# Turning k by 32 by 32 blocks on VectorE and sixteen transfers, in a hash attention kernel with a PReLU MLP behind it

## The chip, the cores and the metric

The kernel runs on one core of a Trainium2 chip. Its engines work side by side, each through its own instructions in order: TensorE (PE: matmuls, and PEld: the loads of their weights), VectorE (DVE), ScalarE (ACT), GpSimd (POOL) and SyncE (SP, which here only issues transfers). They meet through semaphores. Transfers are carried out by 16 DMA engines; an engine that issues one spends time on the issue and goes on, and whoever needs the data waits for the landing. The metric is the device time of one execution in microseconds (us), as the median of several runs. A profile is one execution, recorded instruction by instruction.

## The reference: hash attention, then a two-layer MLP

Four batches of eight heads, 768 positions, head dimension 64. Every q and k row is given six bits, the signs of its products with six columns of `proj`. A query may look only at keys with the same six bits; other scores become -1e9. Then softmax and the product with v. The heads of a batch are put side by side (512 columns) and go through `g = max(h, 0) + alpha * min(h, 0)` with `h = x @ w_in` (512 to 2048), and `out = g @ w_out`.

```python
q_bits = (np.einsum('bhsd,dk->bhsk', q, proj) > 0).astype(np.int64)
mask = q_bucket[:, :, :, None] == k_bucket[:, :, None, :]
scores = np.where(mask, scale * np.matmul(q, k.transpose(0, 1, 3, 2)), -1000000000.0)
```

## The kernel before, in words

Two heads make a pair; there are 16 pairs, and the loop at L1140 takes one per turn. Before the loop the first two pairs are loaded and turned. After it (`attn.close()`, L1201) comes the MLP, which the change does not touch.

Position `p * 6 + c` of a head lies in partition p as its row c, so a natural tile (`qn`, `kn`) holds 128 partitions of six rows of two heads of 64. TensorE needs the 128 numbers of both heads on the partitions and the 768 positions along the free axis. `turn` (L667) makes that: six 128x128 transposes by TensorE into two PSUM banks (L674), and one ScalarE copy out (L679), to `qT` or `kT`. The turned columns come in six groups of 128: group c holds the rows c of all partitions.

`hash_bits` (L687) multiplies the turned q and k by the projection (`hs`, L704), ScalarE's Sign (L710) turns them into `kb`, and six small transfers on SP's queue put the pieces of `kb` where the scores want them: four of 32 rows into `qb` (L715), two of 64 rows within `kb` (L717). `scores` (L734) computes, for each of twelve cells (six groups of keys by two halves of the queries), the bits' product and the score on top of it in one PSUM tile; the weights are 128 columns of `kb` and `kT`, the moving side 384 columns of `qb` and `qT`. ScalarE's exponential (L745) empties the tile into `pt`. `attend` (L767) multiplies `pt` by v into `av`. Meanwhile VectorE adds up the six `pt` tiles (L753, 761, 757, 758, 764), `totals` (L781) sums the partitions with TensorE (`sm`), and `divide` (L794) divides: it runs within the next pair and stores x to DRAM (L823).

In the same loop the MLP's weights are prepared: ScalarE makes `wr` and `wx` of a loaded `raw` piece (`weight_abs`, L580 and L584), VectorE clamps, shifts and adds them (L590, L596, L621, L624), and in some pairs subtracts finished groups (`weight_sums`, L642). Finished groups go back to DRAM (L634, L647). `magnitude` (L681) squares q and k in place and keeps the sum, for a check of range; it is the last use of a natural tile, after which `load` (L499) fills it anew.

The order on TensorE, VectorE, ScalarE and GpSimd is the program's: nearly every instruction is passed to `do`, which keeps it there. Transfers issued on SP are placed by the tile layer by their dependencies. In one turn pi the order is: the scores of pair pi with their exponentials; the division of the pair before; weight work and the sums of `pt`; `hash_bits` of pair pi+1; `turn` of q and of k of pair pi+2; `attend` and `totals` of pi; one `weight_abs`; loads; `magnitude` of q and k of pair pi, each followed by the load for pair pi+3; a second `weight_abs`.

The PSUM tiles named `sc`, `tp`, `hs` and `sm` share three buffers of two banks. Natural tiles of q and k have three buffers each. Each transfer issued by SP or ScalarE takes one of eight semaphores in turn, and its issue waits until the transfer that had this semaphore before has landed.

Of the kernel before, what the change touches and what calls it, by code (L numbers as in the profile page):

```python
# [8 lines left out]
F32 = mybir.dt.float32  # L9
# [398 lines left out]
def fast_path(  # L408
# [12 lines left out]
    nc = tc.nc  # L421
    P = 128
    B, H, S, D = q.shape
# [5 lines left out]
    NC = S // P  # L429
    NK = DM // P  # L430
    NF = DFF // P
    CH = 3
# [44 lines left out]

    pts = [pool.tile([P, NCH, 2, CW + 1], F32, name=f"pt{i}", bufs=1) for i in range(NC)]

    nat, tr, bits = {}, {}, {}  # L480
    accp, accd, av, vsum, sums = {}, {}, {}, {}, {}

# [10 lines left out]
    def load_part(pi, name, cs, queue):  # L493
        b, hp = pairs[pi]
        src = {"q": q, "k": k}[name]
        if cs.start == 0:
            nat[name, pi] = pool.tile([P, NC, 2, D], F32, name=f"{name}n{pi}", tag=f"{name}n", bufs=3)
        for s in range(2):
            queue.dma_start(nat[name, pi][:, cs, s], src[b, 2 * hp + s].rearrange("(p c) d -> p c d", c=NC)[:, cs])  # L499

# [166 lines left out]
    def turn(pi, name, halves=BOTH, engine=None):  # L667
# [10 lines left out]
        else:  # L678
            do(ACT.activation(dst, ps[:, halves, :CW], AF.Copy, scale=DOWN if name == "q" else 1.0))  # L679

    def magnitude(pi, name):  # L681

        t = nat[name, pi].rearrange("p c h d -> p (c h d)")
        n = "qk".index(name)
        do(ACT.activation(t, t, AF.Square, accum_out=mags[:, n, pi : pi + 1]))

    def hash_bits(pi, halves=BOTH, engine=None):  # L687

        if halves.start == 0:
            bits["q", pi] = qbs[pi % 2]
            kb = pool.tile([P, 3 * CW], BF16, name=f"kb{pi}", tag="kb", bufs=1)
            bits["k", pi] = kb[:, :S]
            bits["raw", pi] = kb.rearrange("p (a w) -> p a w", w=CW)
        ps = {"k": two_banks(f"hs{pi}")}
        ps["q"] = psum_av.tile([P, 2, 512], F32, name=f"hsq{pi}", tag="av") if engine is DVE else ps["k"]
        for half in range(halves.start, halves.stop):
            for name in "qk" if engine is DVE else "kq":
                for s in range(2):  # L700
                    r, c = D * s, D * (s ^ half) + 32 * "kq".index(name)

                    for t, c in [("k", c)] + ([("q", c ^ D)] if engine is DVE and name == "q" else []):
                        do(PE.matmul(  # L704
                            ps[t][c : c + 32, half if t == "k" or engine is not DVE else 0, :CW], wh[r : r + D],
                            tr[name, pi][r : r + D, half * CW : (half + 1) * CW], start=True, stop=True,
                        ))
        if engine is None:
            raw = bits["raw", pi]
            do(ACT.activation(raw[:, 0:3:2], ps["k"][:, :, :CW], AF.Sign, bias=hb))  # L710
            for half in range(2):
                for s in range(2):
                    c = D * (s ^ half)
                    cols = slice(half * CW, (half + 1) * CW)
                    nc.sync.dma_start(bits["q", pi][D * s : D * s + 32, cols], raw[c + 32 : c + 64, 2 * half])  # L715
                    if half:
                        nc.sync.dma_start(bits["k", pi][D * s : D * s + D, cols], raw[c : c + D, 2])  # L717
            return
        for half in range(halves.start, halves.stop):
            cols = slice(half * CW, (half + 1) * CW)  # L720
            for s in range(2):
                c = D * (s ^ half ^ (engine is DVE)) + 32
                do(ACT.activation(
                    bits["q", pi][D * s : D * s + 32, cols], ps["q"][c : c + 32, 0 if engine is DVE else half, :CW], AF.Sign, bias=hb[c : c + 32],
                ))

            for to, c, n in [(0, 0, P)] if half == 0 else [(0, D, D), (D, 0, D)]:
                dst, src = bits["k", pi][to : to + n, cols], ps["k"][c : c + n, half, :CW]
                do(DVE.tensor_scalar(
                    dst, src, hb_k[c : c + n, 0:1], hb_k[c : c + n, 1:2], op0=ALU.is_gt, op1=ALU.subtract,  # L730
                ))


    def scores(pi, cells):  # L734
        for kc, g in cells:
            sc = two_banks(f"sc{pi}_{kc}_{g}")
            ks = slice(kc * P, (kc + 1) * P)
            qs = slice(g * CW, (g + 1) * CW)
            for what, first in ((bits, True), (tr, False)):
                for s in range(2):  # L740
                    r = slice(D * s, D * s + D)
                    do(PE.matmul(  # L742
                        sc[:, s, :CW], what["k", pi][r, ks], what["q", pi][r, qs], start=first, stop=not first,
                    ))
            do(ACT.activation(pts[kc][:, g, :, :CW], sc[:, :, :CW], AF.Exp, scale=SCALE / DOWN))  # L745

# [393 lines left out]
    for pi in range(NPAIR):  # L1140
        i = 2 * pi

        def weight_begin():
            weight_clamp(i)
            weight_parts(i)
            add_first(pi)

        scores(pi, [c for c in CELLS if pi or c not in ahead])
        if pi:
            divide(pi - 1, weight_begin)  # L1150
        else:
            add_first(pi)
        weight_sum(i)
        weight_group(i)
        load_weight(i + 3)
        if pi == 0:
            weight_abs(1, DVE)
        weight_clamp(i + 1)
        add_third(pi)
        add_last(pi)  # L1160
        weight_parts(i + 1)
        weight_sum(i + 1)
        weight_group(i + 1)
        load_weight(i + 4)
        add_total(pi)
        weight_sums(2)
        if pi + 1 < NPAIR:
            hash_bits(pi + 1)
        if pi + 2 < NPAIR:
            turn(pi + 2, "q")  # L1170
            turn(pi + 2, "k")
        attend(pi)
        if pi + 1 == NPAIR:
            now = ff1(0, 0)
            now.step(1)
# [12 lines left out]
        if 11 <= pi < 14 or pi == 15:  # L1188
            sum_x(0, min(pi - 11, 3), DVE)
        if pi == 1:  # L1190
            setup_alpha()
        for name in "qk":
            magnitude(pi, name)
            if pi + 3 < NPAIR:
                load(pi + 3, name)
        if pi + 1 < NPAIR:
            weight_abs(i + 3)
# [97 lines left out]
```

## Time and profile before

| | |
|---|---|
| median of three runs | 897.62 us (896.51 to 897.95) |
| the profiled execution | 897.64 us, its span 895.8 us |
| TensorE clock granted | 0.997 |
| busy in the span: PE, PEld, DVE, ACT | 884.2, 598.5, 746.8, 379.5 us |
| attention stage | up to about 341 us |
| first exponential of pairs 1, 8, 9, 10, 11, 14, 15 | 33.04, 178.92, 199.52, 220.13, 240.74, 303.16, 324.11 us |
| chain that ended last | PE 84%, DVE 9%, issue 3%, ACT 2%, DMA 2% |

A row of a group reads: line, engine, operation, tile written from tile read, shapes, count, then busy time in us and the mean of one in ns. A row of a timeline reads: start and duration in us, engine, line, operation, tiles, count, and in brackets how long the engine was idle before and who ended that. Times count from the start of the span. `issue` stands for waiting that no recorded instruction explains. The rows of SPq are its issues, not the data's way.

### The profile page before, as it was taken

To read this page: it belongs to the slowest core of one execution; us is meant where nothing else is said; L and a number is where in the kernel's file an instruction comes from. 1 tells how busy PE (TensorE), PEld (TensorE's weight loads), DVE (VectorE), ACT (ScalarE), POOL (GpSimd) and SP (SyncE) were. 2 spreads that over 40 slices of the span, in tenths; PEclk is the share of its full clock that TensorE was granted. 3 is DMA by queue.
4 is the path that set the end of the run, shared out by engine and by line. 5 is a ranking of instruction groups with operands and counts; after the bars stand their busy time and mean duration, and the time that the engine had idled before them with its cause. 6 is when DMAs were issued, how large, how long until landed. Compare 5 with 4: busy or idle time off the path is not lost.

```text
span 895.8 us, 15331 instructions
## 1 busy us (share of the span) xinstructions
PE 884.2 (99%) x5886; PEld 598.5 (67%) x5886; DVE 746.8 (83%) x1266; ACT 379.5 (42%) x668; POOL 14.4 (2%) x30
## 2 busy tenths in 40 slices
PE   9999999999999999999999999999999999999996
PEld 4544545555555545557997557997557998556996
DVE  5888888888989887899989678988668989768996
ACT  7877777788877762222112222112222111222111
POOL 1000000000000001120000000000000000000000
PEclk9999999999999999999999999999999999999998
DMA  8444575575685625587333435343525242430242
GB/s 235 139 143 129 151 232 153 149 229 173 204 281 163 202 74 185 181 296 289 141 113 107 163 111 166 107 147 88 178 88 192 95 159 80 157 116 0 95 143 72
DMA packets 126177, 137.22 MB, mean 153 GB/s; under 512 B 78976, under 2 KB 110224, under 8 KB 122512
## 3 DMA queue, kind: packets, MB, share of 16 engines
q1 hardware_dynamic: 121376, 126.59, 44.9%
q0 software_dynamic: 2304, 8.39, 2.6%
q10 hardware_dynamic: 2416, 1.18, 0.5%
q8 instruction: 48, 0.79, 0.3%
q14 instruction: 33, 0.27, 0.1%
HBM read 104.87 MB, written 28.31 MB: 149 GB/s over the span
## 4 chain that ended last, share of the span: by engine, by line
PE 84%; DVE 9%; issue 3%; ACT 2%; DMA 2%; SPq 0%; DVEq 0%; ACTq 0%
PE sc L742 12%; PE av L775 10%; PE f_0a L875 2%; PE z_4a L875 2%; PE z_7a L875 2%; PE z_3a L875 2%; PE z_6a L875 2%; PE z_5a L875 2%; PE f_4a L875 2%; PE f_3a L875 2%; PE f_2a L875 2%; PE f_1a L875 2%; PE z_2a L875 2%; PE f_5a L875 2%; DMA qb<-kb 2%
## 5 line engine op out<-in xcount | busy, mean ns | idle before, releaser
L745 ACT ACTIVATE pt<-sc 128x768 f32<-128x768 f32 x192 | 154.8, 812 | 53.5 <-PE sc L742 53.2
L742 PE MATMUL sc<-qT,kT 64*128 64x384 f32 x768 | 155.8, 483 | 0.0
L775 PE MATMUL av<-pt,vn 128*32 128x385 f32 (+1 forms) x1536 | 127.4, 486 | 0.0
L742 PEld LDWEIGHTS sc<-qT,kT 64*128 64x128 f32 x768 | 70.0, 187 | 40.9 <-issue 40.7
L775 PEld LDWEIGHTS av<-pt,vn 128*32 128x32 f32 x1536 | 48.7, 109 | 71.1 <-issue 70.5
L928 DVE TENSOR_TENSOR g<-g,g 128x384 f32<-128x384 f32 x128 | 68.4, 555 | 2.2
L742 PE MATMUL sc<-qb,kb 64*128 64x384 bf16 x384 | 66.5, 323 | 2.4 <-DMA qb<-kb 2.1
L992 DVE TENSOR_TENSOR gs<-g,gs 128x768 f32<-128x768 f32 x56 | 53.3, 952 | 1.0
L992 DVE TENSOR_TENSOR gs<-g 128x768 f32<-128x768 f32 x56 | 53.3, 951 | 0.0
L984 DVE TENSOR_TENSOR ws<-wl 128x512 f32<-128x512 f32 x56 | 38.5, 687 | 17.5 <-DMA wl<-w_out_s 15.9
L753 DVE TENSOR_TENSOR accp<-pt,pt 128x1536 f32<-128x1536 f32 x16 | 28.1, 1759 | 17.5 <-ACT pt L745 17.5
L924 DVE SCALAR_TENSOR_TENSOR g<-h,alpha 128x384 f32<-128x384 f32 x32 | 19.7, 616 | 25.1 <-ACT h L917 25.1
L742 PEld LDWEIGHTS <-kb 64*128 64x128 bf16 x384 | 20.9, 94 | 25.9 <-issue 4.3
L580 ACT ACTIVATE wr<-raw 128x512 int32<-128x512 uint32 x32 | 22.8, 712 | 17.2 <-issue 16.0
L758 DVE TENSOR_TENSOR accd<-accd,pt 128x1536 f32<-128x1536 f32 x16 | 28.1, 1759 | 2.0 <-ACT wr L580 0.5
L761 DVE TENSOR_TENSOR accp<-accp,pt 128x1536 f32<-128x1536 f32 x16 | 28.0, 1753 | 0.0
L757 DVE TENSOR_TENSOR accd<-pt,pt 128x1536 f32<-128x1536 f32 x16 | 28.0, 1752 | 0.0
L764 DVE TENSOR_TENSOR accd<-accd,accp 128x1536 f32<-128x1536 f32 x16 | 28.0, 1751 | 0.0
L805 DVE STREAM_TRANSPOSE st<-sm 128x192 f32<-128x192 f32 x32 | 10.3, 361 | 16.9 <-PE sm L789 16.9
L875 PE MATMUL f_0a<-x,wi 128*128 128x384 f32 x64 | 23.5, 489 | 0.0
L875 PE MATMUL f_4a<-x,wi 128*128 128x384 f32 x64 | 23.3, 486 | 0.0
L875 PE MATMUL f_1a<-x,wi 128*128 128x384 f32 x64 | 23.3, 486 | 0.0
(348 smaller groups left out, 1732.1 us busy)
## 6 DMA issues: line engine op xcount, KB each, us to landing
wi<-w_in_s SPq DMA_DIRECT2D x32, 896.0 KB, 4.7
wl<-w_out_s SPq DMA_DIRECT2D x16, 1024.0 KB, 4.8
wl<-w_out_r SPq DMA_DIRECT2D x12, 1024.0 KB, 4.9
raw<-in_moe_w_out_dram SPq DMA_DIRECT2D x16, 512.0 KB, 3.9
raw<-in_moe_w_in_dram SPq DMA_DIRECT2D x16, 512.0 KB, 4.0
w_in_s<-wsi SPq DMA_DIRECT2D x16, 448.0 KB, 5.8
vn<-in_v_dram SPq DMA_DIRECT2D x16, 384.0 KB, 4.2
x_s<-x SPq DMA_DIRECT2D x16, 384.0 KB, 2.8
```

The lines of the kernel that those rows point to most:

```text
L742: do(PE.matmul(sc[:, s, :CW], what["k", pi][r, ks], what["q", pi][r, qs], start=first, stop=not first,))
L745: do(ACT.activation(pts[kc][:, g, :, :CW], sc[:, :, :CW], AF.Exp, scale=SCALE / DOWN))
L753: do(DVE.tensor_tensor(accp[pi], p(0), p(1), op=ALU.add))
L757: do(DVE.tensor_tensor(accd[pi], p(3), p(4), op=ALU.add))
L758: do(DVE.tensor_tensor(accd[pi], accd[pi], p(5), op=ALU.add))
L761: do(DVE.tensor_tensor(accp[pi], accp[pi], p(2), op=ALU.add))
L764: do(DVE.tensor_tensor(accd[pi], accd[pi], accp[pi], op=ALU.add))
L775: do(PE.matmul(av[pi][D * s + t : D * s + t + 32, g, :w], nat["v", pi][:, s, kc * D + t : kc * D + t + 32], pts[kc][:, g, s, :w], start=(k ...
L875: do(PE.matmul(self.ps[bank], self.left(left, k), self.right(right, k), start=start and k == 0, stop=k == self.nk - 1, skip_group_check=no ...
L928: do(DVE.tensor_tensor(new_g(b, to)[:, i], g_m[b, x][:, i], g_m[b, y][:, i], op=ALU.subtract))
L984: do(DVE.tensor_tensor(t, w2[b, n, x], w2[b, n, y], op=op))
L992: do(DVE.tensor_tensor(t, g2[b, n, x], g2[b, n, y], op=ALU.subtract))
```

## The change

For pairs 2 to 15, k is no longer turned by TensorE. `turn_blocks` transposes the natural tile by VectorE in 32 by 32 blocks, in one instruction of 128x768, into a tile `kB` of one buffer (`tb`), and sixteen transfers on SP's queue move the blocks to `kT`, 32 partitions of 768 bytes each. The columns of such a `kT` stand in the order of the positions, so the group c is every sixth column; `columns` gives the scores this view, with a step of 24 bytes for `kT` and of 12 bytes for `kb`. `hash_bits` reads `kT` in order as before.

The six transfers of the hash bits are issued by ScalarE, directly after the Sign, in place of SP. Natural k tiles have two buffers in place of three. The square of k is that of pair pi+2 in turn pi (turn 0 does those of pairs 0, 1 and 2), so that the tile comes free early. The first two pairs are turned as before.

```diff
-            nat[name, pi] = pool.tile([P, NC, 2, D], F32, name=f"{name}n{pi}", tag=f"{name}n", bufs=3)
+            nat[name, pi] = pool.tile([P, NC, 2, D], F32, name=f"{name}n{pi}", tag=f"{name}n", bufs=2 if name in WITH_DVE else 3)
...
+    def turn_blocks(pi, name):
+        t = pool.tile([P, 4, 32, NC], F32, name=f"{name}B{pi}", tag="tb", bufs=1)
+        do(DVE.transpose(t.rearrange("p b i c -> p b c i"), nat[name, pi].rearrange("p c h (e d) -> p (h e) c d", d=32)))
+        w = NC * 32
+        tr[name, pi] = dst = pool.tile([P, S], F32, name=f"{name}T{pi}", tag=f"{name}T")
+        for a in range(4):
+            for b in range(4):
+                nc.sync.dma_start(
+                    dst[32 * b : 32 * b + 32, a * w : (a + 1) * w],
+                    t[32 * a : 32 * a + 32, b].rearrange("p i c -> p (i c)"),
+                )
+        by_blocks.add((name, pi))
...
+    def columns(what, name, pi, r, c0, c1):
+
+        t = what[name, pi][r]
+        if (name, pi) not in by_blocks:
+            return t[:, c0 * P : c1 * P]
+        t = t.rearrange("p (t c) -> p c t", c=NC)[:, c0:c1]
+        return t[:, 0] if c1 - c0 == 1 else t
...
-                    nc.sync.dma_start(bits["q", pi][D * s : D * s + 32, cols], raw[c + 32 : c + 64, 2 * half])
+                    do(nc.scalar.dma_start(bits["q", pi][D * s : D * s + 32, cols], raw[c + 32 : c + 64, 2 * half]))
                     if half:
-                        nc.sync.dma_start(bits["k", pi][D * s : D * s + D, cols], raw[c : c + D, 2])
+                        do(nc.scalar.dma_start(bits["k", pi][D * s : D * s + D, cols], raw[c : c + D, 2]))
...
-                        sc[:, s, :CW], what["k", pi][r, ks], what["q", pi][r, qs], start=first, stop=not first,
+                        sc[:, s, :CW], columns(what, "k", pi, r, kc, kc + 1),
+                        columns(what, "q", pi, r, CH * g, CH * (g + 1)), start=first, stop=not first,
...
+        if pi == 0:
+            for name in WITH_DVE:
+                magnitude(0, name)
...
-            turn(pi + 2, "k")
+            turn_blocks(pi + 2, "k")
...
-            magnitude(pi, name)
+            for n in [1, 2] if pi == 0 and name in WITH_DVE else [pi + 2 * (name in WITH_DVE)]:
+                if n < NPAIR:
+                    magnitude(n, name)
```

More of the change, by code (lines that the diff above doesn't have):

```diff
@@ L478, in fast_path @@
     pts = [pool.tile([P, NCH, 2, CW + 1], F32, name=f"pt{i}", bufs=1) for i in range(NC)]
+    WITH_DVE = "k"
     nat, tr, bits = {}, {}, {}
@@ L679, in turn @@
             do(ACT.activation(dst, ps[:, halves, :CW], AF.Copy, scale=DOWN if name == "q" else 1.0))
+    def turn_blocks(pi, name):
[10 more added lines that the diff above has]
+        by_blocks.add((name, pi))
+    by_blocks = set()
+    def columns(what, name, pi, r, c0, c1):
[4 more added lines that the diff above has]
+        return t[:, 0] if c1 - c0 == 1 else t
     def magnitude(pi, name):
@@ L736, in scores @@
             sc = two_banks(f"sc{pi}_{kc}_{g}")
-            ks = slice(kc * P, (kc + 1) * P)
-            qs = slice(g * CW, (g + 1) * CW)
             for what, first in ((bits, True), (tr, False)):
```

## The prediction

> **What bounds the kernel now.** I read the page first, for the busy engines, then the tables by stage, the chain of waits, and last the timelines of one pair on four engines, since the change lives wholly in the attention stage (up to 341 us).
>
> ```profile
> PE 884.2 (99%) x5886; PEld 598.5 (67%) x5886; DVE 746.8 (83%) x1266; ACT 379.5 (42%) x668; POOL 14.4 (2%) x30
> 219.10:239.70 20.60, 20.60 (x215) 10.36 (x216) 18.42 (x29) 16.17 (x23) 0.00 (x0) 1.00 0.67 206
> L816 DVE STREAM_TRANSPOSE dn<-rr 128x768 f32<-128x768 f32 x16 | 15.6, 972 | 0.0
> ```
>
> TensorE sets the time: 20.60 us busy of a 20.60 us pair. But VectorE is busy 18.42 of it and ScalarE 16.17, so there is little room beside it. One pair, pair 10, on ScalarE, VectorE, TensorE and the SP queue:
>
> ```profile
> 220.13 9.69 ACT L745 ACTIVATE pt<-sc 128x768 f32<-128x768 f32 x12 [2.95 <-PE sc L742]
> 229.87 0.90 ACT L710 ACTIVATE kb<-hs,hb 128x768 bf16<-128x768 f32 x1
> 231.35 0.81 ACT L679 ACTIVATE kT<-tp_k 128x768 f32<-128x768 f32 x1
> 234.07 0.86 ACT L685 ACTIVATE kn<-kn 128x768 f32<-128x768 f32 x1
> 236.10 0.71 ACT L580 ACTIVATE wr<-raw 128x512 int32<-128x512 uint32 x1 [1.08 <-issue]
> 236.72 0.70 ACT L584 ACTIVATE wx<-raw 128x512 f32<-128x512 f32 x1
> 240.74 0.81 ACT L745 ACTIVATE pt<-sc 128x768 f32<-128x768 f32 x1 [3.31 <-PE sc L742]
> 235.94 1.75 DVE L764 TENSOR_TENSOR accd<-accd,accp 128x1536 f32<-128x1536 f32 x1
> 237.60 1.41 DVE L642 TENSOR_TENSOR wsi<-wsi 128x512 f32<-128x512 f32 x2
> 229.64 0.88 PE L674 MATMUL tp_q<-ident,qn 128*128 128x128 f32 x6
> 230.35 0.82 PE L674 MATMUL tp_k<-ident,kn 128*128 128x128 f32 x6
> 231.10 7.96 PE L775 MATMUL av<-pt,vn 128*32 128x385 f32 x96
> 238.88 0.84 PE L789 MATMUL sm<-accd,ones 128*32 128x192 f32 x16
> 239.65 0.34 PE L742 MATMUL sc<-qb,kb 64*128 64x384 bf16 x2
> 230.79 1.85 SPq L715 DMA_DIRECT2D qb<-kb  x3
> 237.62 1.35 SPq L499 DMA_DIRECT2D qn<-in_q_dram  x2
> ```
>
> Read here: ScalarE rests 3.31 us before the next exponentials, waiting for TensorE: that is its whole slack. VectorE finishes the pair's sums at 239.01, only 1.7 us before those exponentials. SP issues three small transfers in 1.85 us, 0.62 each.
>
> **What the Trainium skill says.** "DMA: Bandwidth & Descriptors", section "Issuing engines are not separate DMA queues": another issuing engine saves only issue time, the 16 DMA engines being shared. The trace shows how much issue time is: 0.62 us each on SP, and four k loads on ScalarE's queue at the start took 2.39 us. "Perfetto Trace Analysis", section "DMA Instruction — HWDGE (DVE, Sync)": the recorded issue ends before the data moves, so a waiter pays the landing too; the trace agrees (0.585 us of issue, 2.4 to landing for qb<-kb). "SBUF — State Buffer", section "Door 1: The DMA port swizzle": successive accesses to new 16-byte lines pay a penalty. The new k is written by VectorE and read as weights at a step of 24 bytes; no row of the trace steps so far (28 output turns step 8 bytes, 556 ns for 384, without visible loss).
>
> **The change, part by part.** It concerns 14 of the 16 pairs. The built order has 84 matmuls fewer and 224 block transfers, so it does what it says.
> *TensorE:* six transposes go, 230.35 to 231.10, 0.75 us a pair, 10.5 in all. Weights of the scores are then strided. They load under matmuls now (187 ns each); twice that would be 2 x 0.374 + 0.19 = 0.94 us a cell and half-array where a cell takes 0.81: at most 1.5 us a pair, at least nothing. I take nothing, because the waits below leave TensorE that room.
> *ScalarE:* the kT copy goes (0.70 of pitch), six issues come, 6 x 0.62 = 3.7 us, between the Sign and the copy of q. They must follow the Sign, and each also waits for the eighth transfer before it in the built order, mostly loads on SP.
> *VectorE:* one 128x768 block turn a pair, after the last sums. The dn row gives 0.97; bounds 0.97 and 1.9 if the step halves it. I take 0.97, since the same instruction with a step of 8 bytes kept pace.
> *SP:* six issues go, sixteen come; same size as qb<-kb (32 rows of 768 bytes), so 16 x 0.62 = 9.9 us a pair. SP then needs about 15 of its 20.6. The bytes, 0.39 MB a pair, raise the DMA share from 0.5-0.9 by under a tenth.
>
> Three new waits decide. In the built order:
> *Chain A, ScalarE behind VectorE.* The square of k (L685) now is that of the pair two ahead, in place on the tile the block turn reads, so it waits for the turn. Behind it stand a wr, a wx and the next twelve exponentials. In pair 10: sums end 239.01, turn 240.0, square 240.9, wr and wx (0.62 + 0.70) 242.3, exponentials at 242.3 instead of 240.74: period 22.2 for 20.61. VectorE's own start depends on the fourth exponential (L753 3.3 us after the first), so the loop closes on itself. In pair 8, without the weight subtractions of L642, sums end 196.48, exponentials at 199.7 instead of 199.52: 20.8. Eight of pairs 1 to 13 have L642: mean 21.7.
> *Chain B, the q load behind the sixteen.* SP issues vn and the next q only after the sixteen: from the turn's end s, 9.9 + 0.65 (vn) + 0.65 to the second q half, which lands 3.5 after: s + 14.8. TensorE's turn of q waits for it, one pair later, and av stands behind it. From tp_q to the exponentials: 0.71 + 7.78 + 0.77 + 1.09 = 10.35. With s 18.6 after the exponentials (19.9 with L642), two periods make 18.6 + 14.8 + 10.35 = 43.75, so 21.9 a pair, 22.5 with L642: mean 22.3. The k blocks themselves, s + 9.9 + 2.4, reach the hash earlier than q does.
> *Chain C, ScalarE behind SP.* In pairs 5, 8 and 11 ScalarE's fifth issue waits for the third store w_in_s that SP issues after the sixteen: 9.9 + 0.65 (vn) + 1.3 (q) = 11.9, two stores of 0.79 and a gap 13.6, x_s and raw 0.4 each, so it starts at s + 14.4 and lands 5.8 (the median of these stores) later. As s is 2.4 before the exponentials (22.3 - 19.9), that is 17.8 after them; two issues (1.2), then qT, wr, wx, qn, kn, wr, wx (4.9) bring the next exponentials at 23.9: 1.6 beyond chain B, three times: 5.
>
> Sum: pairs 1 to 14 start 270.1 us apart now (33.04 to 303.16); 13 x 22.3 = 289.9: +19.8. Chain C +5. Pair 0: only two k tiles now, so the load of k2 waits for k0's square, behind the six issues: Sign 23.5, issues 27.2, square 28.1, load 32.4, turn 33.4, square 34.3, wr and wx 35.7, against 33.04: +2.7. Pair 14, some waiting for stores: +1. The 10.5 us off TensorE and the 2.1 us of TensorE waiting for qb<-kb are already inside these periods: where a chain is longer, the freed time becomes idle TensorE. Together +28.5 on the span 895.8, 924.3; around it 897.64 - 895.8 = 1.8: 926, and the profiled run stands at the median, 897.62. The chains take turns and never help each other, so I say 928. After 341 us nothing changes.
>
> **Rivals.**
> *TensorE keeps the bound (the other side):* if the square's wait were hidden, 895.8 - 10.5 - 2.1 + 1.8 = 885. For it: TensorE 20.60 of 20.60 today. Against: it needs the turn to end 2.2 us before the exponentials at a 19.9 us pair, 17.7 after the last ones; the sums alone end at 17.6 or 18.9 and the turn adds one. It would decide only if chain A were under 20.6 on average. 3 in 100.
> *Chain A alone:* SP issues faster, near the 0.34 of whole-tile stores, or q lands early, so B hides: 13 x 21.7 = 282.1, +12 + 2.7: 912. 20 in 100.
> *The 24-byte step halves the block turn:* +0.97 on A, half on B, some 0.7 x 14: 938. For it the page's note; against, no measured row. 18 in 100.
> *SP becomes the bound:* issues of about 1.0 us (single ones took 1.09 and 1.28) add 6 us to s over two pairs, 3 x 13: 965. 8 in 100.
> *All balance out near no change:* 1 in 100.
> The forecast has 50 in 100, its own range 918 to 936.
>
> **How the numbers follow.** 906 to 950 holds the forecast, nearly all of chain A alone and the halved turn; it leaves out the bound of SP and the gain. Two tenths of a per cent, 1.8 us, is about what a measurement here can tell from no change: faster 0.03, same 0.01, slower 0.96.
>
> **What would show it.** Right: TensorE idle in most pairs before tp_q on a q load, or before sc; ScalarE's square of k waiting on the block turn in every pair, its rest before the exponentials gone; pairs of 21.5 to 22.5 us, the longest at pairs 5, 8, 11; first exponentials of pair 1 near 35.7. Wrong: pairs under 20.6; a turn far from 0.97 us; issues of the k blocks far from 0.62; or tp_q waiting for nothing.

## The result, and the profile after

The changed kernel takes 955.12 us (953.66 to 957.41, four runs) where the one before takes 897.68 in the same comparison: a ratio of 1.0645 [1.0622, 1.0668]. The forecast was 928, with a range of 906 to 950: the sign was right, the size was not, and the time lies outside the range.

The profiled execution has a span of 953.6 us, 57.8 longer than before. The first exponentials of the pairs say where it is. Pair 1 starts at 36.81 us (before 33.04: +3.8). From there to pair 14 it takes 358.30 - 36.81 = 321.5 us (before 270.1: +51.4). Pair 14 takes 23.2 us (before 20.9: +2.3), and from pair 15 to the end it is 572.1 us (before 571.7: +0.4). So nearly all of the loss is in thirteen pairs, 24.7 us each where there were 20.8.

From the page of the changed kernel, its engines; from the table of groups, by shapes, the block turn and the loads of the scores' weights (the last numbers are busy us and ns of one, then the idle time before and who ended it):

```profile
PE 903.4 (95%) x5802; PEld 629.3 (66%) x5802; DVE 767.5 (80%) x1280; ACT 366.2 (38%) x654; POOL 14.4 (2%) x30
L684 DVE STREAM_TRANSPOSE kB<-kn 128x768 f32<-128x768 f32 x14 | 22.4, 1602 | 3.8 <-DMA kn<-in_k_dram 3.8
L764 PEld LDWEIGHTS sc<-qT,kT 64*128 64x128 f32 x768 | 100.0, 293 | 30.5 <-issue 29.9
```

TensorE has 84 instructions less and is busy 19 us longer; a part of this is its clock, which falls where it has to idle (below). The turn takes 1.60 us, not 0.97, and a load of strided weights 293 ns, not 187. The waits of the changed kernel (engine, tile and line waited for; us in all, times, longest):

```profile
ACT qT L680 <- DMA kb<-kb: 34.8, 5, 11.5
ACT qT L680 <- DMA qb<-kb: 28.4, 5, 8.7
PE tp_q L675 <- DMA qn<-in_q_dram: 26.8, 9, 6.2
ACT kn L709 <- DVE kB L684: 14.7, 8, 2.7
```

The last two lines are chains B and A of the prediction. But the largest wait is ScalarE's rest before its copy of q: 86 us in all, where the page of before has none. It is in this time that ScalarE issues its six transfers; the kernel before with those issues and nothing else rests 56 us there (y1 below). The 30 us between them are waits within the issues. Pair 8 shows them, from the timelines of ScalarE, SP and TensorE:

```profile
204.42 9.66 ACT L768 ACTIVATE pt<-sc 128x768 f32<-128x768 f32 x12
215.37 0.90 ACT L734 ACTIVATE kb<-hs,hb 128x768 bf16<-128x768 f32 x1 [1.29 <-PE hs L728]
218.73 3.37 ACTq L739 DMA_DIRECT2D qb<-kb  x3
225.13 0.50 ACTq L741 DMA_DIRECT2D kb<-kb  x1
226.57 0.52 ACTq L739 DMA_DIRECT2D qb<-kb  x1
227.20 0.54 ACTq L741 DMA_DIRECT2D kb<-kb  x1
227.78 0.81 ACT L680 ACTIVATE qT<-tp_q 128x768 f32<-128x768 f32 x1 [11.51 <-DMA kb<-kb]
...
202.48 10.66 SPq L689 DMA_DIRECT2D kT<-kB  x16
213.87 1.30 SPq L500 DMA_DIRECT2D qn<-in_q_dram  x2
215.22 1.63 SPq L648 DMA_DIRECT2D w_in_s<-wsi  x2
218.90 0.47 SPq L567 DMA_DIRECT2D raw<-in_moe_w_in_dram  x1
219.42 1.03 SPq L648 DMA_DIRECT2D w_in_s<-wsi  x1
220.54 1.77 SPq L500 DMA_DIRECT2D kn<-in_k_dram  x2
...
218.79 1.48 PE L675 MATMUL tp_q<-ident,qn 128*128 128x128 f32 x6 [3.46 <-DMA qn<-in_q_dram]
```

The Sign ends at 216.3. In the built order ScalarE's six issues of this pair wait for the eighth transfer before each: the second half of q, two stores w_in_s, a raw load, the third store, the first half of k. All of them are SP's, and all stand behind the sixteen, which end at 213.1. So the first issue goes at 218.7, the fourth at 225.1 when the raw load of 218.9 has landed, the fifth at 226.6 after the store of 219.4, and q is copied 11.5 us after the Sign. Pair 8 is no exception: the trace has each transfer's semaphore and landing, and in the pairs 1 to 13 there are 39 such waits of over 0.1 us, 38.7 us together (more than 30, as an issue after a wait is recorded at about 0.5 us and one after another issue at 0.6). Each ends within 0.1 us after the landing of the transfer of SP that had the same semaphore before. In y1 there is none. The next exponentials start at 232.49, 28.1 us after these. TensorE's wait for q, in the last row, ended 9 us before ScalarE's.

The same stage as a table (stretch, its length, busy time of PE, PEld, DVE, ACT and POOL with instructions, granted TensorE clock, DMA share, GB/s), pairs 7 and 8:

```profile
181.83:204.42 22.59, 21.52 (x216) 12.69 (x214) 20.70 (x36) 15.44 (x23) 0.00 (x0) 1.00 0.52 152
204.42:232.49 28.07, 24.14 (x212) 13.86 (x211) 19.41 (x31) 14.90 (x23) 0.00 (x0) 0.94 0.58 169
```

Pair 7, set by chain A, is about as long as forecast. In pair 8 nothing is busy to the end, and TensorE, which idles, is granted 0.94 of its clock.

Which wait ends last before the next exponentials differs from pair to pair. ScalarE's issues set the pairs 1, 5, 8, 9 and 11 (mean 25.2 us). TensorE's wait for q sets 2, 3, 6, 10 and 12: there ScalarE is done and rests again until the scores come (mean 25.5 us). The square's wait for the turn sets 4, 7 and 13 (mean 22.6 us). The first two feed each other, as pairs 9 and 10 show:

```profile
252.35 0.84 ACT L709 ACTIVATE qn<-qn 128x768 f32<-128x768 f32 x1
253.31 0.55 SPq L500 DMA_DIRECT2D qn<-in_q_dram  x1
254.00 10.31 SPq L689 DMA_DIRECT2D kT<-kB  x16
265.97 0.61 SPq L500 DMA_DIRECT2D qn<-in_q_dram  x1
272.84 1.51 PE L675 MATMUL tp_q<-ident,qn 128*128 128x128 f32 x6 [6.23 <-DMA qn<-in_q_dram]
```

ScalarE, which copied q only 7.4 us after the Sign, squares q at 252.35. SP waits for that before it loads into the same tile; the sixteen go behind this load, and the second half of q behind the sixteen. TensorE waits 6.2 us for it, and pair 10 is the longest of all.

### The profile page after: what moved, and what is told of

Same layout as the page of the kernel before. It is cut to its first block, busy times and chain, and to the rows that moved or that the text cites. A ratio compares the mean times of both kernels' runs of the same rounds, so it can differ in the third digit from the quotient of the medians.

```text
span 953.6 us, 15340 instructions
## 1 busy us (share of the span) xinstructions
PE 903.4 (95%) x5802; PEld 629.3 (66%) x5802; DVE 767.5 (80%) x1280; ACT 366.2 (38%) x654; POOL 14.4 (2%) x30
## 4 chain that ended last, share of the span: by engine, by line
PE 71%; DVE 8%; DMA 8%; ACT 6%; issue 3%; SPq 2%; ACTq 1%; DVEq 0%
PE sc L764 9%; PE av L798 6%; DMA qn<-in_q_dram 2%; ACT pt L768 2%; DMA kn<-in_k_dram 2%; PE z_4a L898 2%; PE f_0a L898 2%; PE z_6a L898 2%; PE z_7a L898 2%; PE z_5a L898 2%; PE z_3a L898 2%; PE f_3a L898 2%; PE f_1a L898 2%; PE f_4a L898 2%; PE f_2a L898 2%
## 5 line engine op out<-in xcount | busy, mean ns | idle before, releaser
L764 PE MATMUL sc<-qT,kT 64*128 64x384 f32 x768 | 167.6, 513 | 0.0
L768 ACT ACTIVATE pt<-sc 128x768 f32<-128x768 f32 x192 | 152.4, 810 | 23.7 <-PE sc L764 17.0
L798 PE MATMUL av<-pt,vn 128*32 128x385 f32 (+1 forms) x1536 | 134.8, 508 | 0.0
L764 PEld LDWEIGHTS sc<-qT,kT 64*128 64x128 f32 x768 | 100.0, 293 | 30.5 <-issue 29.9
L764 PE MATMUL sc<-qb,kb 64*128 64x384 bf16 x384 | 68.8, 329 | 12.6 <-ACT pt L768 4.4
L776 DVE TENSOR_TENSOR accp<-pt,pt 128x1536 f32<-128x1536 f32 x16 | 28.1, 1759 | 29.2 <-ACT pt L768 29.2
L680 ACT ACTIVATE qT<-tp_q 128x768 f32<-128x768 f32 (+1 forms) x17 | 13.1, 772 | 87.2 <-DMA kb<-kb 34.8
L764 PEld LDWEIGHTS <-kb 64*128 64x128 bf16 x384 | 28.3, 119 | 27.1 <-issue 11.3
L675 PE MATMUL tp_q<-ident,qn 128*128 128x128 f32 x96 | 17.5, 330 | 27.9 <-DMA qn<-in_q_dram 26.8
L675 PEld LDWEIGHTS tp_q<-ident,qn 128*128 128x128 f32 x96 | 13.0, 167 | 39.2 <-issue 32.4
L781 DVE TENSOR_TENSOR accd<-accd,pt 128x1536 f32<-128x1536 f32 x16 | 28.1, 1759 | 1.7
L784 DVE TENSOR_TENSOR accp<-accp,pt 128x1536 f32<-128x1536 f32 x16 | 28.1, 1753 | 0.0
L684 DVE STREAM_TRANSPOSE kB<-kn 128x768 f32<-128x768 f32 x14 | 22.4, 1602 | 3.8 <-DMA kn<-in_k_dram 3.8
```

Of the source, the lines that this page charges most:

```text
L675: do(PE.transpose(ps[:, c // CH, c % CH * P :][:, :P], src[:, c], ident))
L764: do(PE.matmul(sc[:, s, :CW], columns(what, "k", pi, r, kc, kc + 1), columns(what, "q", pi, r, CH * g, CH * (g + 1)), start=first, stop=no ...
L776: do(DVE.tensor_tensor(accp[pi], p(0), p(1), op=ALU.add))
L781: do(DVE.tensor_tensor(accd[pi], accd[pi], p(5), op=ALU.add))
L784: do(DVE.tensor_tensor(accp[pi], accp[pi], p(2), op=ALU.add))
L798: do(PE.matmul(av[pi][D * s + t : D * s + t + 32, g, :w], nat["v", pi][:, s, kc * D + t : kc * D + t + 32], pts[kc][:, g, s, :w], start=(k ...
```

## The experiments

All times are medians of four runs or more. "Pairs" is the time from the first exponentials of pair 1 to those of pair 14 in the profiled execution, 13 periods; it isolates what the loop does. In the table C is the changed kernel and B the one before. v3, v4 and u4 leave k's columns in other partitions, so their scores are of other numbers; they show times alone.

| kernel | what it is | us | ratio to before | pairs |
|---|---|---|---|---|
| before | B | 897.7 | | 270.1 |
| after | C | 955.1 | 1.0645 [1.0622, 1.0668] | 321.5 |
| x1 | C, hash bits back on SP | 963.6 | 1.0732 [1.0714, 1.0750] | 332.3 |
| x2 | C, square of k written elsewhere | 960.2 | 1.0691 [1.0673, 1.0709] | 326.9 |
| x3 | C, 8-byte steps | 955.3 | 1.0647 [1.0620, 1.0675] | 319.7 |
| y1 | B, hash bits on ScalarE | 893.8 | 0.9963 [0.9949, 0.9977] | 268.0 |
| x4 | C, sixteen on GpSimd | 937.1 | 1.0434 [1.0388, 1.0481] | 300.6 |
| x5 | C, q load ahead of the sixteen | 945.7 | 1.0540 [1.0521, 1.0559] | 309.9 |
| x7 | x5, square apart, 8-byte steps | 943.3 | 1.0513 [1.0495, 1.0531] | 310.4 |
| x8 | C, turn in mid-pair | 932.2 | 1.0391 [1.0371, 1.0410] | 301.3 |
| v1 | y1, sixteen idle transfers | 954.2 | 1.0620 [1.0596, 1.0644] | 321.0 |
| v3 | C, one transfer for sixteen | 912.5 | 1.0159 [1.0136, 1.0182] | 282.4 |
| v4 | v3, square apart, 8-byte steps | 891.1 | 0.9923 [0.9901, 0.9946] | 264.0 |
| w1 | x8, 8-byte steps, sixteen on GpSimd | 900.0 | 1.0030 [1.0010, 1.0049] | 270.4 |
| v2 | as v1, sixteen ahead of the loads | 924.8 | 1.0308 [1.0285, 1.0332] | 294.6 |
| u2 | C, hash bits on GpSimd | 934.4 | 1.0405 [1.0378, 1.0433] | 304.0 |
| u1 | u2 and x5 together | 924.5 | 1.0289 [1.0264, 1.0313] | 297.6 |
| u4 | v3, square apart | 902.0 | 1.0050 [1.0031, 1.0069] | 274.2 |
| u5 | u1, square apart, 8-byte steps | 924.5 | 1.0302 [1.0274, 1.0330] | 295.8 |

### First round: undo one part at a time

The first theory, Q, was that ScalarE's issues with their waits hold the pair. Its rivals were W, the strided weights and the longer turn, and A, the square's wait. Each run undoes one part of the change; y1 makes one part alone.

x1, the hash bits on SP again:

```diff
-                    do(nc.scalar.dma_start(bits["q", pi][D * s : D * s + 32, cols], raw[c + 32 : c + 64, 2 * half]))
+                    nc.sync.dma_start(bits["q", pi][D * s : D * s + 32, cols], raw[c + 32 : c + 64, 2 * half])
```

> The changed kernel with the six hash-bit transfers back on SP's queue; block turn, sixteen transfers and early square stay. Theory Q (queues: most of the 57 us is ScalarE standing in its issues, which wait for loads that SP issues late behind the sixteen): ScalarE's 87 us of rest before the copy of q falls to about 15, and what is left are the square waiting for the block turn and the q load behind the sixteen: 925 to 935. Theory W (work: the block turn of 1.6 us and the slower strided weights carry the loss): ScalarE's rest only moves elsewhere, 950 to 957.

Measured 963.6: slower than the changed kernel by 8.4 and above both ranges. It looked like the end of theory Q, and was not. ScalarE's rest before the copy of q did shrink, from 86 to 16 us; but the six stand behind the sixteen on SP now, and TensorE waits for them instead (first line). Chain A, the second line, grows from 15 us to 63. From the waits of x1:

```profile
PE sc L764 <- DMA kb<-kb: 17.2, 5, 5.9
ACT kn L709 <- DVE kB L684: 63.2, 13, 6.6
```

Putting a step back where it was does not take its cost away when that queue has been filled in the meantime. The test on a third queue follows in the fourth round.

x2, the square of k no longer in place, so that it need not wait for the turn:

```diff
-        do(ACT.activation(t, t, AF.Square, accum_out=mags[:, n, pi : pi + 1]))
+        do(ACT.activation(to, t, AF.Square, accum_out=mags[:, n, pi : pi + 1]))
...
-                    magnitude(n, name)
-            if pi + 3 < NPAIR:
+                    magnitude(n, name, nat["q", pi] if name == "k" else None)
+        for name in "qk":
+            if pi + 3 < NPAIR:
```

> The changed kernel, but the square of k is written into the used-up q tile and not onto k itself, so that it no longer waits for the block turn. The one wait predicted as chain A is gone, all else stays. If chain A carries the loss as predicted (mean 21.7 to 22.4 us a pair): 935 or less. Theory Q: in most pairs ScalarE is late already from its issues, and the square's recorded wait is only 14.7 us in 8 pairs: 940 to 950. Theory W: no change, 955.

Measured 960.2, above all three expectations. The square's wait is not what sets most pairs; but the edit isn't clean, as the q load, which now follows both squares, is even later. x7 and u5 remove the wait without that.

x3, the columns of k by pairs of rows, so that the steps are 8 bytes instead of 24:

```diff
-        t = pool.tile([P, 4, 32, NC], F32, name=f"{name}B{pi}", tag="tb", bufs=1)
+        t = pool.tile([P, 4, CH, 32, 2], F32, name=f"{name}B{pi}", tag="tb", bufs=1)
...
-        t = t.rearrange("p (t c) -> p c t", c=NC)[:, c0:c1]
-        return t[:, 0] if c1 - c0 == 1 else t
+        t = t.rearrange("p (c t e) -> p c e t", c=CH, e=2)
+        return t[:, c0 // 2, c0 % 2]
```

> The changed kernel with kT's columns in another order, (row pair, partition, row of the pair), so that VectorE writes and TensorE's weight loads step 8 bytes and not 24; the sixteen transfers then move three runs of 256 bytes a partition. Block turn expected near 0.97 us for 1.60, weight loads near 187 ns for 300. Theory W: these two carry the loss, 910 to 920. Theory Q: 14 x 0.63 us on chain A at most and some TensorE time in the scores, so 940 to 948, with ScalarE's rest before the copy of q unchanged near 87 us.

Measured 955.3, no change, outside both ranges. Yet the edit did what it should, as the same two groups of x3 show:

```profile
L684 DVE STREAM_TRANSPOSE kB<-kn 128x768 f32<-128x768 f32 x14 | 13.7, 978 | 4.1 <-DMA kn<-in_k_dram 4.1
L764 PEld LDWEIGHTS sc<-qT,kT 64*128 64x128 f32 x768 | 72.4, 197 | 38.2 <-issue 37.2
```

The step does cost 0.62 us a turn and some 96 ns a load; but here both lie under other waits. (A row of sixteen, now in runs of 256 bytes, takes SP up to 11.9 us instead of 11.1, so a small gain may be hidden.) W falls as the main cause.

y1, the kernel before with the hash bits on ScalarE's queue and nothing else:

> The kernel before with one part of the change alone: the six hash-bit transfers on ScalarE's queue. k is still turned by TensorE. If ScalarE's issues cost by themselves: 6 x 0.62 us against 3.3 us of slack, 0.4 us a pair, 903 to 906. If they cost only together with the sixteen on SP (theory Q: with SP free its loads land before ScalarE has to wait): 896 to 904, ScalarE's rest before the copy of q about 55 us, all of it issue time.

Measured 893.8, a gain of 3.7 us and below both ranges: six issues on ScalarE are harmless where SP is free. From the Sign's end to the copy of q they take 3.8 to 4.7 us in every pair; the pairs of 21.2 to 21.4 us that the kernel before has (pairs 4, 7 and 12) are gone, all run at 20.5 to 20.8.

### Second round: what stands on SP's queue

Common to x1, x2 and x3 are the sixteen on SP, and TensorE waiting for q in all three.

x4, the sixteen on GpSimd's queue (`nc.gpsimd.dma_start` for `nc.sync.dma_start` in `turn_blocks`):

> Theory Q-load (the load of q, issued on SP behind the sixteen block transfers, is late for TensorE's turn of q; that two-pair loop sets the pair in the changed kernel): with the sixteen on GpSimd's queue q is on time. What is left is the loop through the blocks themselves (turn, sixteen issues, landing 1.8, hash 1.2, TensorE to the exponentials 11.6, VectorE 20.5 to the next turn but one): at 0.65 us an issue 45.5 for two pairs, 22.8 a pair, 925 to 940; at 1.0 us an issue 25.6 a pair and about 965, but then with TensorE waiting for kT and no longer for qn. Rival (the transfers as such, wherever they are issued, cost it): TensorE still waits for qn, 950 to 957.

Measured 937.1, in the first range; in the loop TensorE no longer waits for q. What is left is as expected in kind: ScalarE's square waits for the turn (19 us in 9 pairs), and the hash for the last blocks, as this wait of x4 shows.

```profile
PE hs L728 <- DMA kT<-kB: 11.3, 10, 3.0
```

x5, q's square and q's load ahead of the sixteen:

```diff
+        magnitude(pi, "q")
+        if pi + 3 < NPAIR:
+            load(pi + 3, "q")
         if pi + 2 < NPAIR:
             turn(pi + 2, "q")
             turn_blocks(pi + 2, "k")
...
-        for name in "qk":
+        for name in "k":
```

> Only q's square and q's load are moved ahead of the sixteen block transfers in SP's order; all else as in the changed kernel. Theory Q-load: TensorE no longer waits for qn; left are the square of k behind the block turn (22.3 a pair) and the loop through the blocks (22.8 a pair): 922 to 936. Rival (the number of transfers, the lower TensorE clock or the raw loads cost it, not q's place): 945 or more.

Measured 945.7, as the rival had it: q is on time in every pair, and that is worth 9.4 us, no more. The reason shows in the waits: ScalarE rests as before, now in front of q's square.

```profile
ACT qn L709 <- DMA qb<-kb: 68.8, 10, 13.4
```

x7 takes the square's wait and the steps away too; the square goes to a tile of its own.

> As x5_q_ahead, and the square of k is written to a tile of its own (no wait on the block turn), and k's columns lie by pairs of rows (steps of 8 bytes). Theory Q-load: of the three chains only the loop through the blocks stays, 10.4 + 1.8 + 1.2 + 11.0 + 19.9 = 44.3 for two pairs, 22.2 a pair: 910 to 925. If that loop is not there either, TensorE's 20.0 a pair: 885 to 895. Rival as in x5_q_ahead: 940 or more.

Measured 943.3: hardly anything beyond x5. So neither q, nor the square, nor the steps hold it alone; ScalarE's rest (87 us in 12 pairs, `qn` waiting for `qb` and `kb`) does.

x8, the turn and its sixteen from the end of VectorE's pair to its middle:

```diff
+        if 1 <= pi < NPAIR - 2:
+            turn_blocks(pi + 2, "k")
         add_third(pi)
         add_last(pi)
...
-            turn_blocks(pi + 2, "k")
+            if pi == 0:
+                turn_blocks(pi + 2, "k")
```

> The changed kernel with the block turn and its sixteen transfers moved from the end of VectorE's pair to its middle (ahead of the third pair sum), for pairs 3 to 15; square in place, 24-byte steps and all queues unchanged. If the place of the turn in VectorE's order is what makes all the chains (square, q load, blocks), each now has over 5 us of slack and TensorE bounds again at 19.9 to 20.6 a pair (the upper end if the strided weights cost 0.6): 885 to 905. If the number of transfers or SP's total cost it: 940 or more.

Measured 932.2, between the two ranges. Chains A and B are gone, TensorE waits for no q, and still 34 us are lost. ScalarE and SP in one pair of x8:

```profile
206.83 0.90 ACT L734 ACTIVATE kb<-hs,hb 128x768 bf16<-128x768 f32 x1
210.54 4.47 ACTq L739 DMA_DIRECT2D qb<-kb  x3
216.99 0.81 ACT L680 ACTIVATE qT<-tp_q 128x768 f32<-128x768 f32 x1 [9.26 <-DMA kb<-kb]
...
185.17 11.13 SPq L689 DMA_DIRECT2D kT<-kB  x16
204.94 2.17 SPq L500 DMA_DIRECT2D kn<-in_k_dram  x2
208.54 0.38 SPq L567 DMA_DIRECT2D raw<-in_moe_w_in_dram  x1
209.02 11.42 SPq L689 DMA_DIRECT2D kT<-kB  x16
```

By the semaphores, ScalarE's first issue waits for the second half of k, which lands at 210.47, and its second for the raw load of 208.54, which lands at 213.83. Both stand behind the sixteen of the turn before, which end at 196.3. In six of the pairs 1 to 13 ScalarE also waits for some of the sixteen themselves, 9.0 us of 49.1 in all. Theory Q had come back, with a better place: not the issues, but what they wait for.

### Third round: the queue by itself

v1 and v2 add to y1 sixteen transfers a pair that nobody reads; k is turned by TensorE as before.

```diff
         if pi + 2 < NPAIR:
+            idle = dram.tile([16, 32, 192], F32, name=f"idle{pi}")
+            for j in range(16):
+                r = slice(32 * (j % 4), 32 * (j % 4) + 32)
+                some = accd[pi].rearrange("p c w -> p (c w)")
+                nc.sync.dma_start(idle[j], some[r, 192 * (j // 4) : 192 * (j // 4) + 192])
             turn(pi + 2, "q")
```

> The kernel of y1_bits_on_act (k turned by TensorE as before, the hash bits on ScalarE's queue), and per pair sixteen transfers of 32 rows of 768 bytes more on SP at the same place, which nobody waits for (from tiles at hand into DRAM). Theory SP-queue (sixteen issues in a row on SP put the loads behind them by 11 us; that alone makes most of the loss): q is then loaded for TensorE's turn at 17.5 + 11 + 0.6 + 1.3 + 3.4 = 33.8 us after the exponentials where 30.5 is in time; two pairs 17.5 + 16.5 + 12.1 = 46.1, 23.05 a pair, 13 x 2.45 = 32 above 893.8: 915 to 935. Rival (VectorE's turn, the wait of the square or the strided k make the loss): 894 to 900.

v1, where fifteen of the sixteen read the newly loaded k, measured 954.2, above both ranges, and not for the reason given. The built order puts those fifteen behind the load of k, and SP stands until it lands. TensorE then waits for no q at all; ScalarE's rest before the copy of q, 56 us in y1, grows to 130:

```profile
L679 ACT ACTIVATE qT<-tp_q 128x768 f32<-128x768 f32 x15 | 12.2, 810 | 130.5 <-DMA qb<-kb 67.0 <-DMA kb<-kb 33.6 <-PE sm L789 18.5
```

> As v1_sixteen_idle, but all sixteen idle transfers read VectorE's pair sum, so SP issues them in one row from 17.5 us after the exponentials on, ahead of the loads of v, q and k. Theory SP-queue: q late by some 3 us in two pairs and ScalarE's issues held by the k load and the x_s store behind them: 920 to 950. Rival (transfers that nobody waits for cost nothing; VectorE's turn and the strides make the loss): 894 to 905.

v2, the form in the diff, has them in a row ahead of the loads: 924.8, 31.0 above y1 (893.8). So a loss of more than half the size arises without any block turn, square or strided weight. (The sixteen go to DRAM here and take SP 7.3 to 8.8 us a row, less than in the changed kernel.) Its q waits are short (9.2 us in 7 pairs); ScalarE rests 70 us before the copy of q instead of 56.

v3, the other way round: all of the change, but one transfer instead of sixteen.

```diff
-        for a in range(4):
-            for b in range(4):
-                nc.sync.dma_start(
-                    dst[32 * b : 32 * b + 32, a * w : (a + 1) * w],
-                    t[32 * a : 32 * a + 32, b].rearrange("p i c -> p (i c)"),
-                )
+        nc.sync.dma_start(dst, t.rearrange("p b i c -> p (b i c)"))
```

> The changed kernel with one transfer of 128 rows of 3072 bytes per pair instead of sixteen of 32 rows of 768: the same bytes, one issue (k's columns then stand in other partitions, so the scores are of other numbers). Theory SP-queue: the q load, ScalarE's issues and the raw loads are on time; left are VectorE's 1.6 us turn and the square of k behind it, 22.3 a pair: 912 to 926. Rival (the bytes, VectorE's order or the strides make most of the loss): 940 or more.

Measured 912.5, as expected: the same bytes in one issue give back 42.6 of the 57.4 us. It is not the bytes. (One transfer also takes one semaphore where sixteen went twice round the eight; v3 doesn't separate this from the time of the issues.) What is left is chain A, in every pair, 2.0 us at the square:

```profile
ACT kn L704 <- DVE kB L684: 26.1, 13, 2.8
```

v4 removes that wait and the steps.

> As v3_one_transfer (one transfer per pair, the scores are of other numbers), and the square of k written to a dead tile, and k's columns by pairs of rows (8-byte steps). Theory SP-queue: none of the chains is left; TensorE bounds at 20.6 - 0.75 = 19.9 a pair: 882 to 893. If VectorE (18.4 + 1 us, with its waits) bounds instead: 895 to 905. Rival: 915 or more.

Measured 891.1, its pairs 2 to 10 19.6 to 20.4 us. That is what the change, with these two edits, would be worth if k could be moved in one transfer: 6.7 us, of which y1 has 3.7 without it.

u4 stands between the two.

> v3_one_transfer (912.5; one transfer per pair, the scores are of other numbers) with the square of k written to a dead tile: no wait on the block turn; k keeps its 24-byte steps. v4_one_apart_pairs (891.1) has 8-byte steps besides. If the square's wait makes the 21.5 us between the two: 891 to 897. If the strided weights and the longer turn make them: 905 to 912.

Measured 902.0, between the two expectations, so both count: the square's wait 10.5 us of the 21.5, the steps 11.0. The table of u4, one pair with TensorE busy all of the time, shows why a step costs now (columns as above).

```profile
138.10:158.76 20.66, 20.66 (x210) 12.09 (x210) 19.11 (x28) 15.62 (x23) 0.00 (x0) 1.00 0.63 181
```

20.66 in this pair and nearly so in most others, where v4 has 20.0: the slower weights cost nothing in the changed kernel, and 0.65 us a pair as soon as TensorE bounds.

w1 keeps the change's own result: x8 with the steps of x3 and the sixteen on GpSimd.

> The change with its own result kept, with the block turn in the middle of VectorE's pair, k's columns by pairs of rows, and the sixteen transfers on GpSimd's queue. Theory SP-queue: all chains have slack, TensorE bounds at 19.9 a pair: 882 to 893, below the kernel before. If ScalarE's issues still wait for loads as in x8_turn_early: 905 to 925. If GpSimd's transfers land too late for the hash (up to 7.6 us in x4_blocks_on_pool): 895 to 910.

Measured 900.0, in the third range, but not for its reason: the hash waits for the blocks once, 1.4 us. Its pairs from 2 to 10 take 20.4 us each, a little less than before; pairs 0 and 1 take 26.5 and 24.0 (before 23.2 and 20.8), which costs 6.5 us. It does not beat y1, the fastest of the kernels in the table that leave the computation as it was.

### Fourth round: who waits behind the sixteen

u2, the changed kernel with the hash bits on GpSimd's queue, so that ScalarE neither issues them nor waits (`nc.gpsimd.dma_start` in `hash_bits`):

> The changed kernel with the six transfers of hash bits on GpSimd's queue, so that ScalarE neither issues nor waits for SP's transfers. If ScalarE's issues are what holds the pair: 920 to 932 (the square's 22.3 and the blocks' 22.8 a pair are left). If the q load alone holds it: 948 to 956. If both do, each for some pairs: 936 to 948, with TensorE still waiting for qn.

Measured 934.4, 20.7 us less and between two of its ranges. ScalarE's rest before the copy of q falls from 86 to 8 us; most of its rest is now at the square, as chain A has it. TensorE waits for q in two pairs (7.1 us) instead of nine.

```profile
ACT kn L709 <- DVE kB L684: 63.4, 12, 6.6
142.11 1.26 SPq L500 DMA_DIRECT2D qn<-in_q_dram  x2
143.48 12.29 SPq L689 DMA_DIRECT2D kT<-kB  x16
```

But the edit moved more than the hash bits. The tile layer, which places SP's transfers, now puts both halves of q ahead of the sixteen in eleven of fourteen turns, as in the last two lines, where the changed kernel has one or both behind in most. So the 20.7 us are not those of ScalarE's issues alone.

u1 adds x5's earlier q load.

> q's square and load ahead of the sixteen (x5_q_ahead, 945.7) and the hash bits on GpSimd's queue. If the q load and ScalarE's issues are the two takers behind the sixteen: 918 to 934 (the square's and the blocks' loops are left). If a third one, the weight loads for VectorE, holds it: 938 or more.

Measured 924.5, 30.6 less than the changed kernel. The cleaner comparison is with x5: q stands ahead of the sixteen in both, the source differs only in the queue of the hash bits, and SP's order differs little. That queue is worth 21.2 us. With the 9.4 us of q's place (x5) this makes the 30.6. The weight loads are no third of their size.

u5 takes the square's wait and the steps from u1.

> u1_q_ahead_bits_pool (924.5) with the square of k written to a tile of its own and k's columns by pairs of rows; the sixteen transfers stay on SP behind the block turn. If the square's wait and the strides are all that is left: TensorE or VectorE bounds, 20.0 to 20.6 a pair, 888 to 898. If the loop through the blocks holds it: 10.4 + 1.8 + 1.2 + 11.0 + 19.9 = 44.3 for two pairs, 22.2 a pair: 912 to 920. If the weight loads behind the sixteen hold it: above that.

Measured 924.5 again, above the range for the blocks' loop; the pairs take 20.0 to 26.8 us, short and long ones by turns. From the waits and the timeline of TensorE in u5:

```profile
PE hs L729 <- DMA kT<-kB: 16.8, 10, 3.5
151.14 2.03 PE L729 MATMUL hs<-kT,wh 64*32 64x384 f32 x3 [3.15 <-DMA kT<-kB]
```

Now the hash waits for the blocks themselves: the loop turn, sixteen issues, landing, hash, scores, next turn but one. It was worked out at 22.2 us a pair and measures 295.8 / 13 = 22.8. ScalarE also waits for raw loads here (27.3 us in seven pairs for those of w_out), and their share was not separated. Behind the two takers there are thus two more loops of almost the same length, the square's and this one; removing the square's alone shows nothing, and removing this one alone was not tried.

## Why the prediction was wrong, step by step

**What bounds the kernel now; TensorE -0.75 us a pair.** Right. Where no chain is left (v4) TensorE bounds, at about 20.0 us.

**Weights strided: took nothing.** Right for the changed kernel (x3: no difference), because waits cover it. Its price without cover is 0.65 us a pair (u4), inside the bound of 1.5. (v4 and u4 differ by the turn's length too, but in the pair shown TensorE is busy throughout.)

**VectorE's turn: took 0.97, bounds 0.97 and 1.9.** It took 1.60, which the prediction itself had named as a sign of being wrong; the reason for 0.97, that a step of 8 bytes kept pace, did not carry over to 24. The note that the prediction named for the penalty, in the Trainium skill's "SBUF — State Buffer", section "Door 1: The DMA port swizzle", agrees: with the step inside 16 bytes (x3) the same turn takes 0.98. The rival built on this (938) was not the cause, though, since removing the step removed nothing.

**SP: 16 x 0.62 = 9.9 us.** Nearly right: the median issue is 0.59 us, but some are longer, and a row of sixteen takes 10.1 to 11.1 us where the trace shows it whole.

**Chain A, and the rival "chain A alone: 912".** Right in kind: v3, which leaves this chain alone, gives 912.5 and 282.4 us for 13 pairs, where 282.1 was worked out. Some of that is luck, as the turn is 0.6 us longer than assumed.

**Chain B: 22.3 us a pair. Right in kind, too small.** TensorE waits for q in nine pairs, and in five (2, 3, 6, 10 and 12) this wait ends last. Those take 25.5 us in the mean, 16.2 us more in all than five times 22.3. Two terms were too small. The second half of q was to land at s + 14.8 (9.9 + 0.65 + 0.65 + 3.5 makes 14.7); in these pairs it landed at s + 16.3 to s + 20.2. And from the turn of q to the exponentials it took 10.4 to 13.0 us where 10.35 was put, as TensorE's clock falls after the longer waits. Moving q alone (x5) gives 9.4 us back.

**Chain C: "1.6 beyond chain B, three times: 5". This step failed.** The mechanism was named, but for the pairs 5, 8 and 11 and for the third store alone. In pair 8 ScalarE's fifth issue was to go 17.8 us after the exponentials. The turn ended 2.0 us before them (202.42), the store was issued at 219.42, s + 17.0, and the fifth issue went at 226.57, 22.2 us after them. It is late by 4.4 us, mostly a sum of small things: the turn 0.4 later, the sixteen 0.8 longer, the store of x taking 1.9 to issue and not 0.4, the landing some 7 and not 5.8. And it is not three pairs and not one store. ScalarE takes 5.2 to 11.5 us from the Sign to the copy of q in eight of the pairs 1 to 13, because the other semaphores also belong to transfers behind the sixteen: loads of q, k and raw, the store of x. In five pairs this ends last, and they take 14.6 us more in all than five times 22.3, where 5 was put. In others it makes q late, as pairs 9 and 10 show, which the forecast had at nothing. With q ahead of the sixteen in both kernels (x5 and u1), taking the issues from ScalarE is worth 21.2 us. The sentence "they must follow the Sign, and each also waits for the eighth transfer before it in the built order, mostly loads on SP" held the whole cause; the working then priced the issues at 0.62 each and looked for the wait in three pairs only.

**The sum of the thirteen pairs.** 13 x 22.3 = 289.9 and 5 were put; 321.5 was measured. The 31.6 us beyond 289.9 are 14.6 in the pairs that ScalarE's issues set, 16.2 in those that q sets, and 0.8 in the three that chain A sets.

**"The chains take turns and never help each other."** They take turns, as said, but 2 us were put for it. They also lengthen each other: ScalarE late at its issues is late at the square of q, and SP's next load of q waits for that square.

**Pair 0, +2.7, and pair 14, +1.** Measured 3.8 and 2.3. After 341 us nothing changed, as said.

**The signs named beforehand.** The first exponentials of pair 1 came at 36.8, not 35.7. TensorE idle before tp_q on a q load: yes, in nine pairs. The square waiting on the turn in every pair: only in eight, as ScalarE often arrives later than the turn. The longest pairs 5, 8 and 11: they were 10, 8 and 5 (29.6, 28.1, 27.2), with 12 next (27.0).

## What to carry to other kernels

When a change puts a row of issues on a queue, list all that the queue issues after them, and then all who wait for those transfers: readers of the data, and also transfers on other queues that share a semaphore with them. Price every one of these in every pass of the loop, not in the one where it was first seen. And to find the price of a moved step, move it to an idle queue rather than back: back on SP the hash bits cost 8 us more, on GpSimd they cost 21 less (u1 against x5). Then read the built order: in u2 the edit of one queue moved other transfers too.

## What the runs showed of the hardware

Small transfers cost by their number: sixteen of 24 KB take SP 10.1 to 11.1 us to issue, the same 384 KB in one transfer a single issue with 3.0 us to the landing (v3). The prediction drew on the Trainium skill's "DMA: Bandwidth & Descriptors", section "Issuing engines are not separate DMA queues": another engine saves only issue time. In these kernels it does more, since a queue that is held up holds up what is behind it. Six issues a pair on ScalarE cost nothing where SP is free (y1); behind the sixteen, moving them from ScalarE to GpSimd was worth 21.2 us (x5 to u1). In the traces SP and ScalarE draw on the same eight semaphores, and GpSimd's transfers (x4, u2) on eight others; what separate semaphores alone would be worth was not tried. GpSimd issued the block transfers in 0.50 us each (x4, median) where SP took 0.59, but they landed after 3.4 us (up to 7.6) instead of 1.8.

TensorE's granted clock fell with its own idling. In the changed kernel it was 1.00 in the pairs 2, 7 and 9, whose longest wait was 1.1 to 2.2 us, 0.93 or 0.94 in 3, 5, 6 and 8 (2.3 to 3.5 us), and 0.87 to 0.89 in 10 and 12 (6.2 and 4.4 us). Matmuls after the longer waits take longer: the turn of q 1.48 us in pair 8 and 0.85 in pair 9, one of the hash 0.85 us instead of 0.51 after the wait of 3.15 us in u5. So a long wait of TensorE costs more than its length.
